# A gated linear-attention kernel: the output of one chunk and the scores of the next in one visit of the array's quarters, and a stored order of work

## The chip, the core and the metric

The kernel runs on one core of a Trainium2 chip. The metric is the device time of one execution in microseconds (us), lower is better. The core's engines work side by side and wait for each other by semaphores: TensorE (PE in the profile, PEld for its weight loads), VectorE (DVE), ScalarE (ACT), GpSimd (POOL) and SyncE (SP, which here only issues DMAs). TensorE writes its results into the banks of PSUM; the other engines take them from there.

## What is computed

The reference has two parts, one after the other.

```python
# q, k, v, alpha: (4, 8, 768, 48) = batch, heads, steps, head size
for t in range(S):
    state = alpha[:, :, t, :, None] * state + np.einsum('bhd,bhe->bhde', k[:, :, t], v[:, :, t])
    y[:, :, t] = np.einsum('bhd,bhde->bhe', q[:, :, t], state)
x = y.transpose(0, 2, 1, 3).reshape(3072, 384)
h = x @ w_in              # (384, 2048)
g = h - np.tanh(h)
out = g @ w_out           # (2048, 384)
```

The first part is a recurrence with a decay (called gla in the kernel), the second a two-layer network (moe).

## The kernel before

**Units and chunks.** The 3072 rows are cut into 12 units of 256 rows (`NU`), each into two chunks of 128 rows (`CU`). Three units make one batch element, so the state begins anew at units 0, 3, 6 and 9. Unit 0 is computed in one way (`direct`), unit 1 in halves of 64 steps with plain second products, and units 2 to 11 (`u >= PLAIN`) in halves of 64 steps with everything in the quarters of the array.

**One chunk of the recurrence** (units 2 to 11), as tasks on engines:
- `scores` (PE, L812 and L818): 16 products of `kT` and `qT`, 64x64 each, and 16 (8 in the last chunk of a batch element) products of `kn` and the values `vt`, which update the state. Contraction and output are both at most 64 wide, so each uses a quarter of the 128x128 array: one half of its rows (the contraction) and one half of its columns (the output partitions), four of them side by side. They go into the two banks of the tile `sc`, from the pool `ps_sc`, which holds one such tile.
- `masked` (DVE, L829), `mid` and `state` (DVE, L952 and L956), `decay` (DVE, L832): mask the scores into `pm`, bring the state to the chunk's middle and to its end, and decay it for the next chunk.
- `y` (PE, L885 and L895): 16 products of `qT` with the state (`state` for the first half, `mid` for the second; zeros, `none`, where the state begins anew) and 16 of `pm` with `vt`, again in quarters, into another `sc` tile.
- `x` (ACT, L922) and `rest` (DVE, L907): copy y from PSUM into `xT`, and add the part that came out in another place.
- `moves` (SP, L1021): once per unit six small DMAs that put the rows of `xT` in their last place.

**One step of the network** (eight per unit, `FS`): `first` (L1119; from unit 6 on seven products in place of eight, L1130 and L1151) multiplies `xT` with a part of `w_in` into a tile `h`. The pool `ps_h` holds two of these tiles, in turn. ACT and DVE make `g` from `h` (`square` L1162, `cube` L1171, or `keep` L1141/L1143 and `join` L1156 from unit 6 on, then L1166 and L1175), which ends with the tile `h` free again; `sums` (L1188, L1189) prepares seven products in place of eight; `second` (L1199 for units 0 and 1, L1221 after) multiplies `g` with a part of `w_out` into the output's banks. An fp32 product is executed as two matmul instructions, so the profile counts twice as many as the code issues.

**Order.** Every task is given to `Planner.add` with its engine, an assumed duration, a rank and what it must follow. `Planner.run` lists the tasks by a priority on each engine, in eight rounds, with the due times of the best round so far and, from the fifth round on, random noise on them; the best order is recorded, engine by engine, and nothing is reordered after that. Before the first output task, gaps of PE in the plan are filled with idle matmuls (`spin`, L1301), which nobody reads.

**Start.** Unit 0's and 1's inputs are turned by matmuls with the identity (`turn`, L670, 16 products of 64x128 per half of the steps), placed and scanned on DVE (L717, L736), and the weights come in 16 pieces (`fetch`, `read`, L43; ACT L86 and L87, DVE L89 and L90).

Of the kernel before, what the change touches and what calls it, by code (L numbers as in the profile page):

```python
# [9 lines left out]
FP32 = mybir.dt.float32  # L10
# [7 lines left out]
P = 128  # L18
HP = 64
CU = 2  # L20
# [301 lines left out]
class Planner:  # L322
# [5 lines left out]
    ROUNDS, SEED, NOISE = 8, 1, 2.0  # L328
    WITHIN = {"PE": 0.0, "DVE": 0.15, "ACT": 0.1}

    def __init__(self):
        self.tasks = []
        self.last = {}
        self.filler = None
        self.begin = {}

# [4 lines left out]

    def run(self, priority, before, after, late=None, begin=None):


        n = len(self.tasks)
        left = [len(before[i]) for i in range(n)]
        ready, starts, free, open_, choice = [0.0] * n, [0.0] * n, dict(begin or {}), {}, {}

        def choose(e):
            ts = open_[e]  # L350
            at = max(free.get(e, 0.0), min(ready[i] for i in ts))
            best = min((i for i in ts if ready[i] <= at), key=lambda i: (priority[i], i))
            if late:
                end = at + self.tasks[best][2]
                soon = [j for j in ts if at < ready[j] < end and late[j] < min(late[best], end)]
                if soon:
                    j = min(soon, key=lambda j: (late[j], j))
                    fits = [i for i in ts if ready[i] <= at and at + self.tasks[i][2] <= ready[j]]
                    if not fits:
                        return ready[j], e, j  # L360
                    best = min(fits, key=lambda i: (priority[i], i))
            return at, e, best
        for i in range(n):
            if not left[i]:
                open_.setdefault(self.tasks[i][1], []).append(i)
        order, stale = [], set(open_)
        while any(open_.values()):
            for e in stale:
                choice.pop(e, None)
                if open_.get(e):  # L370
                    choice[e] = choose(e)

            at, engine, i = min(choice.values())
            open_[engine].remove(i)
            starts[i] = at
            free[engine] = at + self.tasks[i][2]
            order.append(i)
            stale = {engine}
            for j, lat in after[i]:
                ready[j] = max(ready[j], free[engine] + lat)  # L380
                left[j] -= 1
                if not left[j]:
                    open_.setdefault(self.tasks[j][1], []).append(j)
                    stale.add(self.tasks[j][1])
        assert len(order) == n
        return starts, order

    def order(self):
# [10 lines left out]
        chance = random.Random(self.SEED)  # L399
        priority, late, best = [t[3] for t in self.tasks], None, None  # L400
        for n in range(self.ROUNDS):
            starts, order = self.run(priority, before, after, late if n % 2 else None, self.begin)
            ends = [s + t[2] for s, t in zip(starts, self.tasks)]
            if best is None or max(ends) <= best[0]:
                best = max(ends), starts, order
                turned, _ = self.run([-e for e in ends], after, before)
                back = [r + t[2] for r, t in zip(turned, self.tasks)]
                fair = [max(back) - b for b in back]
            late = fair if n < 4 else [x + chance.gauss(0, self.NOISE) for x in fair]
            priority = late  # L410
        _, starts, order = best
        plan = sorted(((starts[i], n, self.tasks[i][5], i) for n, i in enumerate(order)), key=lambda x: x[:2])
# [15 lines left out]
def fast(tc, q, k, v, alpha, moe_w_in, moe_w_out, out, w_in, w_out, ident, ok, pad_rows):  # L428
    nc = tc.nc
    B, H, S, D = q.shape  # L430
    NP = H // 2
# [15 lines left out]
    with ExitStack() as ctx:  # L447
# [74 lines left out]
        s_gap = raw_pool.tile([P, KT, 2 * gap], FP32, name="s_gap", bufs=1)  # L522
# [24 lines left out]
        def head(g, r):  # L547

            return 2 * g + (r + (g >= NP // 2)) % 2
# [30 lines left out]
        def load(u, what):  # L582
# [20 lines left out]
            for r in range(2):  # L603
                src = x[b].rearrange("h s d -> h (s d)")[:, t0 * D:(t0 + TU) * D]
                for g in (0, NP // 2):
                    nc.sync.dma_start(out=t[HP * r:HP * r + 32, g:g + 2].rearrange("p g t d -> p g (t d)"),
                                      in_=src[head(g, r):head(g, r) + 3:2].rearrange("g (i n) -> i g n", i=32))

        def gla(u, rank):
# [18 lines left out]
            for what, name in enumerate(("aT", "kT", "qT", "v")):  # L628
                go(f"load {name}", "SP", 1.3 if direct or what == 3 or by_matmul(u, what) else 2.2, -9 + 0.1 * what,
                   [what < 3 and u > 0 and not by_matmul(u - 1, what) and not by_matmul(u, what) and f"{name}{prev}"]  # L630
                   + [u == 1 and ("kUba 0" if what == 3 else "turn qTb 0")]
                   + [f"{last} {u - 2}.{CU - 1}" for last in ("y", "state") if what == 3 and u > 1
# [23 lines left out]
            def turn(what, n):  # L656

                if what == 2:
                    if "both" not in m:
                        m["both"] = two_banks()  # L660
                    t = m["both"][:, n]
                elif what == 1 and u == 0:
                    t = ps_h.tile([P, NP, P], FP32, name="turned", tag="h")
                else:
                    t = ps_o.tile([P, NP, P], FP32, name="turned", tag=f"o{2 * u + n}")
                m["turned", what, n] = t
                for g in range(NP):
                    for r in range(2):
                        at = (head(g, r) * CU + n) * D
                        T.matmul(t[HP * r:HP * r + HP, g, :], lhsT=rough[u, what][:, at:at + HP], rhs=ident,  # L670
                                 start=True, stop=True)

            def turned(what, n):
                return m["turned", what, n].rearrange("p g (c i) -> p g c i", c=CU)

            def place(n):
                (V.tensor_copy if n else A.copy)(tail.rearrange("p g c (i two) -> p g c i two", two=2)[:, :, :, :, n],
                                                 turned(0, n))

            def times(what, by, n, cs):  # L680

                name = ("aT", "kT", "qT")[what]
                if name not in m:
                    new(name)
                to, of = (x.rearrange("p g c (i two) -> p g c i two", two=2)[:, :, cs, :, n] for x in (m[name].rearrange("p c g t -> p g c t"), gc(m[by][:, :, 1:])))
                V.tensor_mul(to, turned(what, n)[:, :, cs], of)

            later = u > 0
            for n, ab in enumerate("ab"):
                if by_matmul(u, 0):  # L690
                    go(f"turn aT{ab}", "PE", 0.92, n * 0.1, ["load aT", later and "masked 0.0"], lambda n=n: turn(0, n))
                    go(f"aT{ab}", "DVE" if n else "ACT", 0.62, 0, [f"turn aT{ab}"], lambda n=n: place(n))
                if by_matmul(u, 1):
                    go(f"turn kT{ab}", "PE", 0.92, 1 + n * 0.1,
                       ["load kT"] + [later and x for x in ("x 0.0", "y 0.1", "state 0.1")], lambda n=n: turn(1, n))
                    for x, _, cs in parts:
                        go(f"kU{ab}{x}", "DVE", 0.33 if x else 0.6, 3, [f"turn kT{ab}", f"U{x}", n and f"kUa{x}", later and "back 0.1", later and by_matmul(u, 2) and "turn qTb"],
                           lambda n=n, cs=cs: times(1, "U", n, cs))
                if by_matmul(u, 2):
                    go(f"turn qT{ab}", "PE", 0.92, 2 + n * 0.1,  # L700
                       ["load qT"] + [later and f"qW{x}{y} 0" for x in "ab" for y in "ab"], lambda n=n: turn(2, n))
                    for x, _, cs in parts:
                        go(f"qW{ab}{x}", "DVE", 0.33 if x else 0.6, 5, [f"turn qT{ab}", f"W{x}", n and f"qWa{x}", later and "y 0.1", later and by_matmul(u, 1) and "turn kTb"],
                           lambda n=n, cs=cs: times(2, "W", n, cs))
            for what, (name, k_) in enumerate((("aT", 0), ("kT", 2), ("qT", 4))):
# [3 lines left out]
                go(name, "DVE", 1.9, k_, [f"wide {name}"] + ([f"y {u - 2}.{CU - 1}"] if u > 1 else []),  # L709
# [37 lines left out]
            def done(by, what):  # L747

                return lambda u, c=None: [f"{by}{ab}{x} {u}" for ab in "ab" for x in ("ab" if c is None else "ab"[c])
                                          if u == 0 or x == "a"] if u == 0 and by_matmul(u, what) else (  # L750
                    [f"{by}{ab} {u}" for ab in "ab"] if by_matmul(u, what) else [f"{by} {u}"])
            kU, qW = done("kU", 1), done("qW", 2)
            for x, ns, _ in parts:
                go(f"U{x}", "DVE", 1.13 if x else 2.2, 1, (["aTa", "aTb"] if by_matmul(u, 0) else ["aT"])
# [660 lines left out]
```

## Time and profile before

| what | us |
|---|---|
| three timed runs | 569.62, 570.61, 570.75; median 570.61 |
| the profiled execution, its own time | 571.14 |
| its span, from the first to the last instruction | 569.4 |
| matmuls L1119, L1130, L1151 (first product), busy | 133.1 + 130.7 + 49.4 |
| matmuls L1221, L1199 (second product), busy | 245.0 + 44.2 |
| matmuls L812, L818 (scores), busy | 15.2 + 25.2 |
| matmuls L885, L895 on sc (y), busy | 22.1 + 25.2 |

Busy times of PE rows overlap: a matmul lasts longer than the time after which the next one starts, so they add up to more than the span. The chain of waits and the timeline, where the start of the next row ends a row, show what a stretch of matmuls takes. The granted TensorE clock was 0.998 of full speed.

### The profile page before, as it was taken

Reading aid. Unit: us, or ns where it says so; the run is one execution under the profiler, and the core shown is the slowest. Engines: PE = TensorE matmul, PEld = TensorE weight load, DVE = VectorE, ACT = ScalarE, POOL = GpSimd, SP = SyncE. Lnnn points to the kernel's source line nnn. Section 1 sums busy time; section 2 is a strip of 40 time slices with the busy share of each in tenths; the row PEclk is TensorE's granted clock in tenths of the full one; section 3 lists DMA queues with packets and bytes.
Section 4 is the critical chain, followed back from the end, with each engine's and each line's share of the span. In section 5 each row is a group of like instructions: output and inputs, shape, how many; then the busy total and the mean of one; then the engine's idle time right before and its main releaser. Section 6 shows DMA issues by size and latency. Waiting matters only on the chain.

```text
span 569.4 us, 14498 instructions
## 1 busy us (share of the span) xinstructions
PE 556.5 (98%) x5881; PEld 504.2 (89%) x5881; DVE 480.8 (84%) x883; ACT 360.0 (63%) x703; POOL 4.8 (1%) x23
## 2 busy tenths in 40 slices
PE   8989999999999999999999999999999999999895
PEld 8877677778998999998999999899999999999894
DVE  6799889999998996895996999899999766776763
ACT  2788976648786676585685665585655455454650
POOL 3000000000000000000000000000000000000000
PEclk9999999999999999999999999999999999999999
DMA  7888852256652762562530311311200100100001
GB/s 192 213 246 229 283 135 62 69 122 138 145 117 77 132 159 88 120 163 91 165 103 15 91 31 29 89 32 29 62 4 1 33 5 1 35 3 0 29 1 35
DMA packets 60716, 50.88 MB, mean 89 GB/s; under 512 B 35776, under 2 KB 50400, under 8 KB 60640
## 3 DMA queue, kind: packets, MB, share of 16 engines
q1 hardware_dynamic: 57728, 48.88, 33.2%
q10 hardware_dynamic: 2912, 0.98, 0.7%
q8 instruction: 48, 0.79, 0.6%
q14 instruction: 28, 0.23, 0.2%
HBM read 44.04 MB, written 4.72 MB: 86 GB/s over the span
## 4 chain that ended last, share of the span: by engine, by line
PE 94%; DVE 2%; ACT 1%; issue 1%; DMA 1%; SPq 0%; POOL 0%; DVEq 0%; ACTq 0%; POOLq 0%
PE o L1221 32%; PE h L1119 22%; PE h L1130 13%; PE o L1199 7%; PE h L1151 7%; PE sc L812 2%; PE sc L885 2%; PE sc L818 2%; PE sc L895 2%; PE spin L1301 1%; PE sc L998 1%; PE turned L670 1%; DVE same L1280 1%; DMA raw<-in_moe_w_in_dram 1%; SPq L43 0%
## 5 line engine op out<-in xcount | busy, mean ns | idle before, releaser
L1119 PE MATMUL h<-xT,w_in 128*128 128x256 f32 x576 | 133.1, 381 | 0.8 <-ACT xT L927 0.5
L1119 PEld LDWEIGHTS h<-xT,w_in 128*128 128x128 f32 x576 | 107.5, 190 | 16.9 <-ACT xT L927 0.7
L1221 PE MATMUL o<-b,e 128*128 128x192 f32 x480 | 94.9, 326 | 0.0
L1221 PEld LDWEIGHTS o<-b,e 128*128 128x128 f32 x480 | 80.1, 190 | 0.8
L1221 PE MATMUL o<-w_out,e 128*128 128x192 f32 x320 | 79.7, 331 | 0.0
L1221 PE MATMUL o<-b,g 128*128 128x192 f32 x320 | 70.4, 326 | 0.0
L1175 DVE SCALAR_TENSOR_TENSOR g<-z,w 128x512 f32<-128x512 f32 x96 | 65.5, 684 | 4.2 <-ACT z L1166 1.2
L1143 ACT COPY u<-h 128x128 f32<-128x128 f32 x96 | 25.2, 263 | 63.1 <-PE h L1130 62.7
L1166 ACT ACTIVATE z<-u 128x512 f32<-128x512 f32 x96 | 60.4, 630 | 2.1
L1162 ACT ACTIVATE u<-h 128x512 f32<-128x512 f32 x48 | 28.4, 592 | 46.7 <-PE h L1119 46.6
L1221 PEld LDWEIGHTS o<-w_out,e 128*128 128x128 f32 x320 | 55.2, 190 | 2.3
L1130 PE MATMUL h<-xT,w_in 128*128 128x128 f32 x288 | 56.2, 280 | 1.1 <-DVE w L1156 0.9
L1130 PE MATMUL h<-xT,w_out 128*128 128x128 f32 x288 | 55.9, 276 | 1.3 <-ACT u L1141 1.3
L1221 PEld LDWEIGHTS o<-b,g 128*128 128x128 f32 x320 | 53.8, 190 | 0.2
L1156 DVE TENSOR_TENSOR w<-h,u 128x512 f32<-128x512 f32 x48 | 32.9, 686 | 23.5 <-PE h L1151 23.1
L1181 ACT ACTIVATE big<-u 128x1024 f32<-128x1024 f32 x48 | 50.3, 1049 | 0.0
L1130 PEld LDWEIGHTS h<-xT,w_in 128*128 128x128 f32 x288 | 47.5, 190 | 3.0 <-DVE w L1156 1.5
L1151 PE MATMUL h<-xT,w_in 128*128 128x256 f32 x192 | 49.4, 380 | 0.0
L1130 PEld LDWEIGHTS h<-xT,w_out 128*128 128x128 f32 x288 | 45.8, 191 | 2.1 <-ACT u L1141 1.5
L1188 DVE TENSOR_TENSOR e<-g 128x384 f32<-128x384 f32 x80 | 43.9, 549 | 1.8
L1162 ACT ACTIVATE u<-w 128x512 f32<-128x512 f32 x48 | 30.3, 630 | 23.1 <-DVE w L1156 22.2
L1199 PE MATMUL o<-w_out,g 128*128 128x384 f32 x128 | 44.2, 489 | 0.0
(158 smaller groups left out, 874.3 us busy)
## 6 DMA issues: line engine op xcount, KB each, us to landing
raw<-in_moe_w_out_dram SPq DMA_DIRECT2D x16, 768.0 KB, 4.9
raw<-in_moe_w_in_dram SPq DMA_DIRECT2D x80, 96.0 KB, 4.1
raw<-in_moe_w_in_dram SPq DMA_DIRECT2D x16, 288.0 KB, 4.7
vt<-in_v_dram SPq DMA_DIRECT2D x23, 192.0 KB, 3.7
ar<-in_alpha_dram SPq DMA_DIRECT2D x44, 96.0 KB, 3.0
kr<-in_k_dram SPq DMA_DIRECT2D x40, 96.0 KB, 2.3
qr<-in_q_dram SPq DMA_DIRECT2D x40, 96.0 KB, 2.2
out_dram<-cross SPq DMA_DIRECT2D x19, 96.0 KB, 1.7
```

The source lines that it names most:

```text
L1119: T.matmul(h[:, a, :], lhsT=w_in[:, j, f * P:(f + 1) * P], rhs=xT[u][:, j, :], start=(j == 0), stop=(j == KT - 1))
L1130: T.matmul(m["h", s][:, to], lhsT=left[n][:, s], rhs=right[u][n], start=start, stop=True, skip_group_check=True)
L1143: A.copy(m["kept", s][:, n], m["h", s][:, 3])
L1151: T.matmul(m["h", s][:, 2 * a:2 * a + 2].rearrange("p i t -> p (i t)"), lhsT=wi[:, KT - 1, s, a], rhs=xT[u][:, KT - 1, :], start=False, st ...
L1156: V.tensor_add(m["w", s], m["h", s].rearrange("p i t -> p (i t)"), m["u", s])
L1162: A.activation(m["u", s], m["h", s], AF.Square, scale=W_SCALE ** -1.5)
L1166: A.activation(m["z", s], m["u", s], AF.Square, bias=QB, scale=QA * W_SCALE)
L1175: V.scalar_tensor_tensor(out=g.rearrange("p a c t -> p (a c t)"), in0=m["z", s], scalar=QK, in1=m["w", s], op0=ALU.add, op1=ALU.mult)
L1181: A.activation(big, m["us", s // 2].rearrange("p s t -> p (s t)"), AF.Relu, bias=-U_FAST, scale=W_SCALE, accum_out=over[:, n:n + 1])
L1188: V.tensor_sub(e[:, 0:3, :], x[:, 3:4].to_broadcast([P, 3, P]), x[:, 0:3])
L1199: T.matmul(m["o"][c], lhsT=g[:, a, c, :], rhs=w_out[:, f, :], start=(f == 0), stop=(f == FT - 1))
L1221: T.matmul(o[n][:, i], lhsT=g_, rhs=w_, start=(s_ == 0 and (n, i) in ((0, 0), (1, 0), (2, 1), (3, 0))), stop=(s_ == FS - 1), skip_group_ch ...
```

## The change

1. **One visit for two tasks.** For units 2 to 11 the task `y` of a chunk is no longer a task of its own: `visit((u, c), py)` issues the y of the chunk before (`py`) together with the scores of chunk `(u, c)`. The first scores of unit 2 have no y beside them, and the y of the last chunk of all stands alone, so there are 19 joint visits. Each row half of the array has its own list, two products of one and two of the other are issued in turn: rows 64 to 127 begin with y, rows 0 to 63 end with it. Between the two parts of y that go to the same bank stands a wait for the last product of the first part.
2. **Where y goes.** Most of y goes into a tile of `ps_h`, the pool of the first product (`m["yb", c]`); the rest into columns that the scores leave free in the two banks of `sc` (`lone`). `x` is two ACT copies from the first, `rest` one DVE copy from the second, in place of two additions; `rest` no longer waits for `x`.
3. **Zero state.** Where the state begins anew, y leaves out the products with `none`.
4. **Heads.** Head `NP * r + g` takes the place of `head(g, r)` before, so both row halves write the same column halves. `products` for unit 0, `halves_products` and the loads follow.
5. **Start.** `turn` uses quarters (32 products of 64x64 per tensor instead of twice 16 of 64x128); unit 0's second y is cut into `carried` and `y`; the very first `first` is cut into two halves of 128 rows.
6. **Order.** The listing is replaced by a stored list, `STEPS`: the whole order of all tasks. The plan's times come from walking through it with the assumed durations, and are used for `spin`, of which there are 36 instead of 24. The DMAs on SP are as many as before (571); the first two pieces of `w_in` no longer stand next to each other, unit 1's inputs come between them.

```diff
-            return 2 * g + (r + (g >= NP // 2)) % 2
+            return NP * r + g
...
+        def visit(of_s, of_y):
...
+            both = two_banks()
...
+            if of_y:
+                open_y[of_y](both, work, first)
+            if of_s:
+                open_s[of_s](both, work)
+            apart = not of_s
+            (own0, y0, s0), (own1, y1, s1) = work[0], work[1]
+            rows0, rows1 = own0 + s0 + y0, y1 + own1 + s1
+            if apart:
+                rows0 = [None] * len(y1) + rows0
+            before = last = None
+            for k in range(0, max(len(rows0), len(rows1)), 2):
+                for rows, mine in ((rows1, y1), (rows0, y0)):
+                    for do in rows[k:k + 2]:
+                        if do is None:
+                            continue
+                        if mine is y0 and y0 and do is y0[0]:
+                            tc.add_manual_dep(T.nop(nofuse=True).ins, last.ins.name, mybir.DependencyInfo(
+                                mybir.DependencyClass.Sync, mybir.DependencyReason.DATA), reason="one bank, two row tiles")
+                        it = do()
+                        if mine is y1 and y1 and do is y1[-1]:
+                            last = it
...
+                def s_work(both, work):
...
+                                work[r][2].append(lambda g=g, x=x, s=s, r=r, q=q: T.matmul(
+                                    flat[r][s, g * HP:(g + 1) * HP], lhsT=m["kT"][q, c, g, s], rhs=m["qT"][q, c, g, s],
+                                    start=True, stop=True))
...
+                def y_work(both, work, begun):
...
+                    bank = m["yb", c] = ps_h.tile([P, NP, P], FP32, name="h")
...
+                    for t in range(2):
+
+                        own, ys, _ = work[t]
+                        for e in range(NP // 2):
+                            for x in range(n == 0, 2):
+                                for hh in range(2):
+                                    (own if x == t and e == 0 else ys).append(carried(t, e, x, hh))
+                        for r in range(2):
+                            for e in range(NP // 2):
+                                for hh in range(2):
+                                    (own if r == t and e == 0 else ys).append(within_(r, e, t, hh))
...
+                    if u >= PLAIN:
+
+                        t = xT[u][0:ROWS, 0:1, c * P:c * P + HP]
+                        to = bass.AP(t.tensor, t.offset, [t.ap[0], (2 * TU + HP, 2), (1, HP)])
+                        V.tensor_copy(to, m["y", c].rearrange("p r g t -> p r (g t)")[0:ROWS, :, NP * (HP + D):])
+                        return
...
-                        both = m["y", c][2]
-                        A.copy(xT[u][0:ROWS, :, to].rearrange("p (a b) t -> p a b t", a=2), both[0:ROWS, :, 0:2, :])
+                        bank = m["yb", c]
+                        A.copy(xT[u][0:ROWS, 1::2, to], bank[0:ROWS, 1::2, :])
+                        t = xT[u][0:ROWS, 0:1, c * P + HP:c * P + 2 * HP]
+                        to = bass.AP(t.tensor, t.offset, [t.ap[0], (2 * TU - HP, 2), (1, HP)])
+                        t = bank[0:ROWS, 0:1, HP:2 * HP]
+                        A.copy(to, bass.AP(t.tensor, t.offset, [t.ap[0], (2 * P - HP, 2), (1, HP)]))
...
+                    go_c("scores", "PE", 2.23 if py else 1.27, 7, kU(u, c) + qW(u, c) + [f"natural {u}", f"load v {u}"] + [x for x in held if x in plan.names()],
+                         lambda: visit((u, c), py))
...
+                    if (u, c) == (NU - 1, CU - 1):
+                        go_c("y", "PE", 1.9, 9, [f"{x} {me}" for x in ("masked", "mid", "decay")] + [f"rest {past}"], lambda: visit(None, (u, c)))
...
+                for g in range(NP):
+                    for n in range(CU):
+                        for c, x in enumerate(halves):
+                            for r in range(2):
+                                at = (head(g, r) * CU + n) * D
+                                T.matmul(m["turned", what, c][HP * r:HP * r + HP, g, :, n], lhsT=rough[u, what][x, at:at + HP], rhs=ident[x, x],
+                                         start=True, stop=True)
...
-                    go_c("y", "PE", 1.6 if n == 0 else 2.9, 9,
-                         ["masked", f"load v {u}", n > 0 and "decay", "gaps"], products)
+                    if n > 0:
+                        go_c("carried", "PE", 1.4, 8.5, ["decay", "gaps"] + qW(u, c), lambda: products(True))
+                    go_c("y", "PE", 1.6, 9, ["masked", f"load v {u}", n > 0 and "carried", "gaps"], lambda: products(False))
...
+                elif u == s == 0:
+                    add(f"first_a {me}", "PE", 1.35, r, [f"in{s}", bank, "x 0.0"], lambda: first(slice(0, P)))
+                    add(f"first {me}", "PE", 1.35, r, [f"first_a {me}", "x 0.1"], lambda: first(slice(P, TU)))
...
+        order, at = [], 0
+        for step in self.STEPS.split():
+            at += int(step)
+            order.append(at)
```

## The prediction, made before the changed kernel was run

> **What bounds the kernel.** I read the busy shares first, then the stages, then the chain of waits. The page's first row, and the table of stages (start:end, length, busy us of PE, PEld, DVE, ACT, POOL, clock, DMA share, GB/s):
>
> ```profile
> PE 556.5 (98%) x5881; PEld 504.2 (89%) x5881; DVE 480.8 (84%) x883; ACT 360.0 (63%) x703; POOL 4.8 (1%) x23
> ...
> 0.00:40.00 40.00, 36.36 (x460) 32.47 (x460) 31.05 (x60) 23.95 (x40) 4.83 (x23) 1.00 0.84 218
> 40.00:150.00 110.00, 109.97 (x1090) 83.98 (x1091) 104.52 (x173) 83.88 (x138) 0.00 (x0) 1.00 0.57 149
> 150.00:350.00 200.00, 200.00 (x2166) 185.62 (x2165) 175.82 (x325) 134.94 (x260) 0.00 (x0) 1.00 0.41 103
> 350.00:562.00 212.00, 209.60 (x2167) 201.87 (x2166) 168.25 (x327) 117.20 (x268) 0.00 (x0) 1.00 0.08 22
> ```
>
> From 40 to 562 us PE is without work for 0.03 + 0 + 2.4 us, at full clock. So there the time is the sum of what PE is given, and work of DVE and ACT counts only if PE comes to wait for it. Only the first 40 us have slack (36.36 busy, of it 8.1 idle matmuls, row L1301), and the last 7 are the output.
>
> What does a visit to the array's quarters take? Busy times overlap, so I take starts from the chain of waits (start us, us until the next piece, what):
>
> ```profile
> 42.89 0.62 PE y L885 x32
> 43.51 0.47 PE y L895 x31
> 43.98 0.47 PE sc L812 x32
> 44.45 0.45 PE sc L818 x26
> 44.90 2.78 PE o L1199 x8
> 47.68 2.59 PE h L1119 x12
> 50.27 2.58 PE o L1199 x8
> 52.85 0.62 PE y L885 x32
> 53.47 0.47 PE y L895 x31
> 53.94 2.79 PE h L1119 x12
> ...
> 93.69 0.62 PE sc L812 x32
> 94.32 0.44 PE sc L818 x26
> 94.76 2.79 PE h L1119 x12
> ```
>
> The reader is to see three visits. y alone: 53.94 - 52.85 = 1.09, and the full-array matmuls after it take 2.79 in place of 2.59, so 1.29. Scores alone: 94.76 - 93.69 = 1.07 + 0.20 = 1.27. And at 42.89, in unit 1, y and scores happen to follow each other: 44.90 - 42.89 = 2.01, + 0.20 (2.78 against 2.58) = **2.21**. Inside a visit 32 executed matmuls take 0.47, or 14.6 ns each; 0.15 is lost on entering (0.62 against 0.47) and 0.2 on leaving. Two tasks in one visit save one entry and one exit: 1.29 + 1.27 - 2.21 = 0.35. The change does by design what the order did once by chance.
>
> **The change, part by part.**
>
> *Joint visits, 19.* Each keeps all its products (the program's order shows 64, executed as 128) and saves 0.35. New is the wait of y's second part for its first, PE on itself. The order shows 16 products, 32 executed, between the two, which is 0.47 of work, while one matmul lasts 0.217 (row L895): it should be over when PE gets there. Behind it queue the last 12 products of y and 12 of the other row half, and then the network. Bounds: 0, or a full drain, 0.22 for the matmul and 0.05 for a semaphore instruction (51 ns in PE's queue rows). I take 0.05, the instruction, since the work between covers the rest: 19 x (0.35 - 0.05) = **-5.7**.
>
> [...] The new order puts two products of the same row half next to each other[...]. But L895 and L818 already run in such pairs, and take 0.47 and 0.44 for 32, no more than L812, which changes row halves each time. The row decides: no cost. [...] L885 before lets both row halves write one bank in turn, in different column halves, at full rate; now the column halves are the same. [...]
>
> *Zero state.* 24 products with zeros go, executed 48 (row "sc<-qT,none" x48): 48 x 14.6 ns = **-0.7**, at three visits.
>
> *The last y alone.* Its parts now follow each other: 12 positions with one row half, 4 with both, 12 with one. A position takes what 4 executed matmuls take side by side, 58 ns: 28 x 0.058 + 0.35 + 0.05 = 2.0 in place of 1.29: **+0.7**.
>
> *x and rest.* ACT: two copies of 112x256 and 112x128 (354 and 272 ns, row L927) in place of one of 581 (L922): +0.05 per chunk. DVE: one copy of 112x128, nearest row L912 (282), in place of 2 x 417 (L907): 20 x 0.55 = -11 us. Neither is on the path (DVE 84%, ACT 63%), so 0; DVE becomes freer, which helps the waits below.
>
> *The tile h for y.* y holds one of the two tiles until x has copied it (0.63), so first products stand closer behind the tile they take over. Adding up PE's work in the two orders between the last use of a tile and its next, the least is 3.7 us before and 2.07 now among plain steps, 1.5 in both among seven-product steps. Release needs square 0.59 and cube 0.68, or join 0.69, and hand-overs: about 1.5 and 0.9. Covered, by less: 0, and up to 0.2 per visit, 4 in all, where ACT is behind.
>
> *moves.* The last y of a unit now comes in the next unit's first visit. Its six DMAs (about 0.45 each in issue, 1.8 to landing), x, rest and from unit 6 on mix (4 x 0.29) make some 7 us; PE has 10 us of other work there where it is tightest (units 2 and 7, by the order). SP has as many DMAs as before. 0.
>
> *Order.* The gaps to win are the 2.4 above. One as the chain shows it:
>
> ```profile
> 532.89 0.56 DVE same L1280
> 533.45 0.61 DVE w L1171
> 534.06 0.03 issue
> 534.08 0.02 DVEq L1175
> 534.11 0.04 issue
> 534.15 0.70 DVE g L1175
> ```
>
> Here PE waits while DVE does the output first; 361 is like it. A longer search may remove these or open others: from -2.4 to +4; I take **-1.2**.
>
> *Start.* Followed through DVE: the turned input is complete about 0.9 earlier (one tensor of 32 quarter products in place of two halves), but the masks of unit 0 still end at about 21; its second y, shorter by the part issued before, then stands behind a turn, so its copy ends later than before (27 against 24.6), and the piece `in1` comes later on SP and DVE. On the other side three turns and unit 1's first scores lie earlier. The third first ends at about 40 in both: **-0.2**, within 2 us either way.
>
> **Sum**: -5.7 - 0.7 + 0.7 - 1.2 - 0.2 = -7.1. Span 569.4 -> 562.3, the profiled execution 571.14 -> 564.0. The timed median lies 0.5 below that execution: 570.61 -> **563.5**.
>
> **Rivals.**
> 1. *The visit drains.* If the wait costs 0.27 at all 20 places, 4.4 of the gain go: 568. For: the order of y and of the row halves has not been seen on the chip. Against: 0.47 of work between. 10%.
> 2. *The shared tile decides: slower.* ACT also has pieces of 1.05 + 0.19 (L1181). If one stands ahead of square whenever y has taken the other tile, release takes 2.7 against the least cover of 2.07, 0.65 of wait at each of 19 visits: 12.3 against 7.1 of gain, so 576. It decides from 7.1 / 19 = 0.37 per visit. Against: most covers are larger (median 7 in plain steps). 7%.
> 3. *The visits bring nothing*, because the new order opens as many gaps as they close, in the start above all: 570.5. 4%.
> 4. *More than summed*: all 2.4 of gaps go, the wait is free and the start wins 2: -7.1 - 1.2 - 1.0 - 1.8 = 559.5. 10%.
>
> **Chances.** The forecast with its own range (560 to 567) has 69%. Two executions of one kernel differ by up to 0.2%, about 1.1 us, which is no change. Faster: 69 + 10 + 10 = 89%. Same 4%, slower 7%. For 8 in 10, with rival 1 and most of 4: 559 to 568.5.
>
> **What would show it.** The chain has y and scores as one stretch of about 2.05 to 2.1, with one 2.79 (or its like) after it; no PE wait on itself of over 0.1 in a visit; PE over 99% busy from 40 us on; `rest` at 0.28. I am wrong if first products wait for cube, join or the copies x, if a visit takes over 2.4, or if the first output product starts over 2 us later than at 44.9.

## The result, and the profile after

| | us |
|---|---|
| before, four timed runs | 569.62 to 570.75, median 570.61 |
| after, four timed runs | 565.16 to 566.20, median 565.92 |
| ratio after to before | 0.9919, 95% interval 0.9902 to 0.9937 |
| forecast | 563.5, range 559.0 to 568.5 |
| span of the profiled execution, before and after | 569.4 and 564.5 |

The change makes the kernel 4.7 us faster where 7.1 were forecast. The page's first row, the row of the granted clock and the table of stages (same columns as before):

```profile
PE 553.1 (98%) x6029; PEld 502.9 (89%) x6029; DVE 463.9 (82%) x855; ACT 358.7 (64%) x723; POOL 4.9 (1%) x23
...
PEclk9989999999999999999999999999999999999998
...
0.00:40.00 40.00, 36.22 (x645) 31.51 (x646) 29.79 (x55) 19.68 (x34) 4.92 (x23) 0.96 0.77 200
40.00:150.00 110.00, 110.00 (x1139) 84.50 (x1140) 102.45 (x167) 87.98 (x147) 0.00 (x0) 1.00 0.57 155
150.00:350.00 200.00, 199.87 (x2147) 187.56 (x2147) 165.45 (x309) 131.50 (x264) 0.00 (x0) 1.00 0.41 102
350.00:557.00 207.00, 206.25 (x2099) 198.89 (x2098) 164.79 (x326) 119.53 (x280) 0.00 (x0) 1.00 0.09 24
```

From 40 us on PE is idle for 0 + 0.13 + 0.75 us, where it was 0.03 + 0 + 2.4. New is the 0.96 in the first row: the clock was not full there. The chain of waits (start, us until the next piece, what) around one joint visit:

```profile
181.99 1.08 PE h L1242 x5
183.07 0.19 PE h L975
183.27 0.05 PE h L975 x2
...
185.06 0.03 PE h L975
185.08 3.94 PE o L1344 x23
```

L975 is now y, in both of its places. From 183.07 to 185.08 are 2.01 us, and the 0.2 of leaving makes 2.21. All 16 joint visits with a state take that to within 0.01; the three where the state begins anew take 1.98, and the last y alone 2.08. Before, y took 1.29 and scores 1.26, each by itself. So 19 x (1.288 + 1.261 - 2.214) = 6.4 come from the visits, 3 x 0.23 = 0.7 from the zeros, and 0.8 are given back by the last y: **-6.3**. The gaps bring **-1.6**. These make -7.9, and the span fell by 4.9; about 3 went elsewhere. The chain at the start shows where:

```profile
33.14 0.97 DVE w_in L89
...
34.15 4.56 PE h L1242 x12
...
38.82 0.97 DVE w_in L89
...
39.84 2.86 PE h L1242 x12
42.69 0.62 PE sc L853 x32
...
44.96 2.79 PE h L1242 x12
47.74 2.58 PE o L1322 x8
```

The first output product starts at 47.74, not at 44.90: **+2.8**. The second first product (34.15) takes 4.56 us where its twins take 2.8. The trace's clock records say why: PE is at full clock from 6.94 us, at half from 34.24 to 37.66, and at full again from there to 559.90, past PE's last matmul. Before the half clock, PE had stood idle twice, for 0.37 and 1.58 us (timeline; in brackets the idle time before a row, and what ended it), the second time until the piece `in1` of the weights was converted (33.14):

```profile
31.97 0.60 PE L1121 MATMUL y<-ident,kT 112*128 112x112 f32 x4 [0.37 <-DVE kT L729]
34.15 4.54 PE L1242 MATMUL h<-xT,w_in 128*128 128x256 f32 x12 [1.58 <-DVE w_in L89]
```

The next piece was converted only when the long product was over (38.82), so the 1.7 lost there stay lost. -6.3 - 1.6 + 2.8 = -5.1, against 4.9 of the span.

### The profile page after: what moved, and what is told of

Same layout as the page of the kernel before. It is cut to its first block, busy times and chain, and to the rows that moved or that the text cites. A ratio compares the mean times of both kernels' runs of the same rounds, so it can differ in the third digit from the quotient of the medians.

```text
span 564.5 us, 14803 instructions
## 1 busy us (share of the span) xinstructions
PE 553.1 (98%) x6029; PEld 502.9 (89%) x6029; DVE 463.9 (82%) x855; ACT 358.7 (64%) x723; POOL 4.9 (1%) x23
## 4 chain that ended last, share of the span: by engine, by line
PE 94%; DVE 3%; issue 1%; ACT 0%; POOL 0%; DVEq 0%; ACTq 0%; POOLq 0%
PE o L1344 32%; PE h L1242 22%; PE h L1253 13%; PE o L1322 7%; PE h L1274 7%; PE h L975 4%; PE spin L1428 2%; PE sc L948 2%; PE sc L1121 1%; PE sc L955 1%; PE sc L975 1%; PE turned L717 1%; DVE same L1407 1%; DVE W L779 0%; DVE U L760 0%
## 5 line engine op out<-in xcount | busy, mean ns | idle before, releaser
L1242 PE MATMUL h<-xT,w_in 128*128 128x256 f32 (+1 forms) x588 | 132.9, 380 | 1.7 <-DVE w_in L89 1.6
L1242 PEld LDWEIGHTS h<-xT,w_in 128*128 128x128 f32 x588 | 109.8, 192 | 18.0 <-DVE w_in L89 2.7
L1344 PEld LDWEIGHTS o<-b,e 128*128 128x128 f32 x480 | 78.8, 191 | 0.2
L1344 PE MATMUL o<-b,g 128*128 128x192 f32 x320 | 68.4, 326 | 0.0
L1279 DVE TENSOR_TENSOR w<-h,u 128x512 f32<-128x512 f32 x48 | 32.9, 686 | 36.7 <-PE h L1274 36.7
L1253 PE MATMUL h<-xT,w_out 128*128 128x128 f32 x288 | 54.1, 275 | 0.0
L1253 PEld LDWEIGHTS h<-xT,w_in 128*128 128x128 f32 x288 | 48.4, 190 | 4.2 <-DVE w L1279 1.5
L1274 PE MATMUL h<-xT,w_in 128*128 128x256 f32 x192 | 49.0, 380 | 0.0
L1294 DVE TENSOR_TENSOR w<-h,u 128x512 f32<-128x512 f32 x48 | 32.7, 680 | 15.0 <-ACT u L1285 15.0
L1253 PEld LDWEIGHTS h<-xT,w_out 128*128 128x128 f32 x288 | 44.3, 192 | 0.1
```

The source lines that it names most:

```text
L1242: T.matmul(h[:, a, to], lhsT=w_in[:, j, f * P:(f + 1) * P], rhs=xT[u][:, j, to], start=(j == 0), stop=(j == KT - 1))
L1253: T.matmul(m["h", s][:, to], lhsT=left[n][:, s], rhs=right[u][n], start=start, stop=True, skip_group_check=True)
L1274: T.matmul(m["h", s][:, 2 * a:2 * a + 2].rearrange("p i t -> p (i t)"), lhsT=wi[:, KT - 1, s, a], rhs=xT[u][:, KT - 1, :], start=False, st ...
L1279: V.tensor_add(m["w", s], m["h", s].rearrange("p i t -> p (i t)"), m["u", s])
L1294: V.tensor_mul(m["w", s], m["h", s], m["u", s])
L1344: T.matmul(o[n][:, i], lhsT=g_, rhs=w_, start=(s_ == 0 and (n, i) in ((0, 0), (1, 0), (2, 1), (3, 0))), stop=(s_ == FS - 1), skip_group_ch ...
```

## The experiments

What was open: whether the gain is that of the visits or of the searched order; whether the wait inside a visit is free or covered; and what the start lost. All runs are set against the kernel before on the same chip, whose median was 570.98 to 571.66 there.

**The changed kernel again**, on one chip with three of the runs below (both edits together, both pieces earlier, every visit split).

> The changed kernel itself, as the base on one chip for the runs beside it. Theory A (the half clock of its profiled execution[...]): some executions are at a mean clock of 0.999 and about 1 us shorter; median 565.9. Rival B (it always happens): all executions at a clock of 0.993 to 0.994.

Measured: 565.01 (563.50 to 565.43), ratio 0.9896 (0.9874 to 0.9918). With the first four there are nine executions. Five have a mean clock of 0.993 or 0.994, and times of 565.13 to 566.20 (mean 565.7); four have 0.997 to 0.999, and 563.50 to 565.16 (mean 564.5). The one with the half clock in its records had 0.993, and 3.41 us at half of a span of 564.5 are 0.003. So by an estimate from the mean clocks the half clock comes in some executions, as theory A has it, and these take 1.2 more on the mean; why in those alone was not shown. Of the kernel before, 3 of the 37 executions beside the runs below are at 0.993 or 0.994. The execution profiled here, at 0.997, is one without the half clock at this place:

```profile
33.40 2.87 PE h L1242 x12
...
37.40 2.86 PE h L1242 x12
40.26 0.62 PE sc L853 x32
...
42.27 2.79 PE h L1242 x12
45.05 2.58 PE o L1322 x8
```

From the second first product to the third are 4.00 us, against 5.69 in the other execution: 1.69 are the half clock. The visit of unit 1 takes 42.27 - 40.26 = 2.01, against 2.27. The same two waits of PE stand before 33.40 (0.38 and 1.59 us), and here the product behind them takes 2.87.

The remaining 0.75 arise at the very start. In the first execution the records of full clock begin at 6.94 us, so most of the first turn lies before them; it takes 1.89 us there and 1.16 here (first execution, then this one):

```profile
5.28 1.89 PE L717 MATMUL turned<-ident,rough 64*64 64x64 f32 x64
```

```profile
5.19 1.16 PE L717 MATMUL turned<-ident,rough 64*64 64x64 f32 x64
```

That is 0.73, and what follows on PE keeps the lead, up to 33.40 against 34.15. The first output product starts at 45.05, about as before the change (44.90). But in the kernel before the records of full clock begin at 6.92, as late as in the first execution; with as slow a turn the changed one would be at about 45.8 (an estimate: 45.05 + 0.75). The span is 561.8, 7.6 under that of before, but it compares the fastest of nine executions with one (571.14) that was slower than the four timed ones beside it. The medians on this chip, 565.01 and 570.98, are 6.0 apart.

**Matmuls in the idle time.**

```diff
+                    for _ in range(7 if (u, s) == (0, 1) else 0):
+                        T.matmul(h[:, 0, 0:P], lhsT=ident, rhs=ident, start=True, stop=True)
                     for a in range(2):
                         f = 2 * s + a
```

> Seven matmuls of the identity stand in front of first 0:1, where TensorE was without work for 1.58 us and the clock then fell to half for 3.4 us. Theory A (the half clock is a cost of its own at the start: 12 matmuls at 380 ns in place of about 216): first 0:1 takes 2.6 in place of 4.56 us, the first output product starts about 1.9 earlier, at 45.8 in place of 47.74, and the time falls by 1.9 to 564.0. Rival B (the start is bound by the conversions of w_in on VectorE and ScalarE, whatever the clock): first 0:1 is shorter, but what follows waits for the conversions; 565.9, no change.

Measured: 564.01 (563.90 to 565.10), ratio 0.9887 (0.9864 to 0.9911), all executions at 0.997 to 0.999.

```profile
31.97 0.60 PE y L1121 x4
32.58 1.58 PE h L1240 x14
...
34.16 2.87 PE h L1244 x12
...
45.81 2.58 PE o L1324 x8
```

L1240 are the added matmuls. The product behind them starts at the same time and takes 2.87 instead of 4.56, and all that follows is 1.9 earlier (45.81 against 47.74). In the profile theory A holds. The median is 1.9 under that of the changed kernel's first four executions (565.92), but only 1.2 under that of all nine (565.16), of which only five are at 0.993 or 0.994.

**The order of unit 1's visit.** Before the change y stood ahead of the scores there, after it behind them. The edit, in the decoded order:

```diff
+        order.remove(names["y 1.0"])
+        order.insert(order.index(names["scores 1.1"]), names["y 1.0"])
```

> In unit 1 alone, y 1.0 stands before scores 1.1, as it did in the kernel before. Theory A (scores before y cost 2.46 in one visit, y before scores 2.21): the time falls by 0.25, to 565.7, and the visit at 42.6 us takes 2.21. Rival B (the 2.46 came from something else, such as the start of the row halves at different times): the visit still takes about 2.45 and the time does not move.

Measured: 564.47 (563.70 to 564.89), ratio 0.9889 (0.9871 to 0.9907), the visit 2.01 + 0.20. Theory A falls all the same: the changed kernel, with the scores first, also takes 2.01 + 0.20 when it is run again. All six executions are at 0.996 or 0.997; in the profiled one the same two waits of PE (0.37 and 1.58 us) stand before the second first product, and it takes 2.86. The 2.46 belongs to that one execution. The profiled execution of the split visits below has a long one in that place too (2.55, a visit that was not split), also behind a slow product (4.54 us); why is open.

**Both of the last two.**

> The changed kernel with two edits: seven matmuls of the identity where first 0:1 waits, and y 1.0 before scores 1.1. Theory A (each saves its own: the half clock in the executions where it falls, some 1 on the median, and 0.25): 1.2 to 1.5 below the changed kernel beside it, and all executions at 0.997 or more. Rival B (one of the two is nothing[...]): as the changed kernel less 1.0 at most.

Measured: 564.42 (563.89 to 564.85), 0.6 under the changed kernel beside it, at 0.996 to 0.999. The ratio is 0.9887 (0.9865 to 0.9909), that of the matmuls alone: the swap adds nothing, as rival B has it.

**The weight piece earlier.** `read in1` moved ahead of `sizeU 1`, `in1` ahead of `W 1`, `first 0:1` ahead of `back 1`, in the same way as above.

> The piece in1 is read and converted before the sizes and the second scan of unit 1, and first 0:1 stands before back 1. Theory A (the order of the start is what was mis-sized: in1 lands at about 25.5 us but is read only at 29, and first 0:1 starts at 34.15): first 0:1 starts at about 31, nothing runs at half clock, the first output product starts at about 45, and the time falls by 2.5 to 3, to 563. Rival B (the order only passes the wait on: unit 1's scans come 1.5 us later on VectorE and the scores of unit 1 wait in its place): 565 to 566.

Measured: 565.48 (564.08 to 566.42), ratio 0.9906 (0.9880 to 0.9932), which is the changed kernel's own. Rival B has the time right, but not what waits:

```profile
34.23 0.41 ACT kn L1135
...
36.02 1.06 ACT more L86
...
37.11 0.97 DVE w_in L89
...
38.13 4.25 PE h L1248 x12
```

`first 0:1` runs early now, but `back 1` comes behind it, so ScalarE's copy of it (L1135) comes later, and the reading of the next piece `in2` (L86) stands behind that copy in ScalarE's queue. PE waits 2.5 us for `in2`, and the product behind it takes 4.25 us where its twins take 2.86; the mean clock from 0 to 40 us is 0.97 here.

**All three edits of the start.**

> The three edits of the start together: in1 early, the seven matmuls of the identity, y 1.0 before scores 1.1. Theory A (what the start lost, 2.7 us, is order and clock, and nothing later takes it up): the first output product starts at 44.5 to 45, and the whole gain reaches the end: 563.0. Rival B (from 45 us on the kernel waits for weight pieces or for VectorE, so that an earlier start is taken up later): less than 1 of it reaches the end, over 565.

Measured: 567.51 (566.47 to 568.34), ratio 0.9940 (0.9921 to 0.9959): slower than the changed kernel. The added matmuls stand in front of `first 0:1`, which now finds its input ready, so they delay it and `back 1`, and `in2` with them: PE waits for it until 39.71, where without them it was 38.13, and the product behind takes 4.54 us. The 1.6 between are what the seven matmuls took.

**Both pieces earlier.** `read in2` ahead of `square 0:0` and `in2` ahead of `cube 0:0`, with the moves of the two orders above and no added matmuls.

> Both pieces in1 and in2 are read and converted ahead (read in1 before the sizes of unit 1, read in2 before square 0:0, so neither stands behind natural 1), first 0:1 before back 1, y 1.0 before scores 1.1. Theory A (the early order failed only because in2 stood behind natural 1 on ScalarE): first 0:1 at 31, first 0:2 at about 36, the first output product at 43 to 44 and the time 1.5 to 2 below the swap with warm clock beside it, about 562. Rival B (the start is bound by VectorE's work as a whole, so that masks, state or in3 come later by what in2 comes earlier): the first output product at 45 or later, about 564.

Measured: **562.27** (562.02 to 563.26), ratio 0.9853 (0.9831 to 0.9875), 2.7 under the changed kernel on that chip and 2.2 under the two edits. It is the fastest of all, and theory A holds. The first output product on the timeline (start, us, engine, line), in this kernel and in the changed one run beside it, the mean clock of the first 40 us 1.00 in both:

```profile
43.28 2.74 PE L1334 MATMUL o<-w_out,g 128*128 128x384 f32 x8
```

```profile
44.89 2.74 PE L1322 MATMUL o<-w_out,g 128*128 128x384 f32 x8
```

1.6 earlier, and nearly all of it reaches the end (spans 560.3 and 561.8). So the start was not bound by VectorE's work as a whole but by the order of these tasks in the queues of VectorE and ScalarE.

**Every visit split.** One matmul of the whole array stands in the middle of each of the 19 visits.

```diff
+                if k == 12 and of_s and of_y:
+                    T.matmul(flat[1][:, NP * HP:NP * HP + 16], lhsT=ident, rhs=ident[:, 0:16], start=True, stop=True)
                 for rows, mine in ((rows1, y1), (rows0, y0)):
```

> In each of the 19 joint visits one matmul of the whole array, 16 columns, stands after 48 products of the 64 or fewer, so that entering (0.15) and leaving (0.2) are paid twice; everything else, the order too, stays. Theory A (the gain of a joint visit is one entry and one exit): each visit takes 2.55 to 2.65 in place of 2.21, and the time rises by 19 x 0.35 to 0.42 = 6.7 to 8. Rival B (the visits bring little and the gain came from the searched order): under 2 more.

Measured: 574.39 (572.01 to 576.04), ratio 1.0062 (1.0044 to 1.0079), 9.4 above the changed kernel on that chip.

```profile
184.83 0.19 PE h L977
...
185.68 0.33 PE sc L632 x2
186.01 0.19 PE sc L977
186.20 0.06 PE sc L977 x2
...
187.32 2.80 PE o L1346 x16
```

The visit takes 187.32 - 184.83 = 2.49 in place of 2.01, so 0.48 more: 0.33 from the added matmul (L632) to the next one, which holds the leaving and its own work, and 0.15 for entering once more (one product takes 0.19 where the two behind it take 0.06). 19 x 0.48 = 9.1. Theory A holds: what a joint visit saves is an entry and an exit. The price is above the 0.42 given; the added matmul's own time is in it and was not measured apart. With the order unchanged, the gain is gone and more: the visits carry it.

**The wait uncovered.**

```diff
-            rows0, rows1 = own0 + s0 + y0, y1 + own1 + s1
+            rows0, rows1 = own0 + s0[:8] + y0 + s0[8:], y1 + own1 + s1
```

> In every joint visit the second part of y stands right behind the last product of the first part (8 products of the scores that stood between them come after it), so that TensorE's wait on itself has 2 products of cover in place of some 16. Theory A (the wait is a drain of one matmul and a hand-over, 0.22 + 0.05, and was free only because of the products between): each visit takes 2.4 in place of 2.21 and the time rises by 19 x 0.2 = 4, from 565.0 on this chip's kind to 569. Rival B (the wait costs nothing in any place[...]): 565, no change.

Measured: 569.73 (569.15 to 570.45), ratio 0.9964 (0.9950 to 0.9978).

```profile
182.80 0.19 PE h L975
...
183.66 0.10 PE sc L975 x4
183.76 0.05 issue
183.81 0.26 PE h L975 x2
...
185.14 3.94 PE o L1344 x23
```

At 183.76 PE waits, and the next two products take 0.26 where two of them take 0.04 elsewhere: with the issue and a longer step before it, about 0.3 more. The visit is 2.34 + 0.19 = 2.53 in place of 2.21, and 2.18 in place of 1.98 where the state is new: 16 x 0.32 + 3 x 0.20 = 5.7. The median rises by 4.7 against 565.01, but that was on another chip, and two of the five executions there are at 0.994 where all of these are at 0.997 or more; against the four of the nine at 0.997 or more (564.5) it is 5.2. So the wait is real and costs more than the 0.27 I gave for a full drain; in the changed kernel, with 16 products of the scores before it, it is free.

**The changed kernel in an order that is not searched long.** The listing of the kernel before replaces the stored list. It got one more rule, that a task takes a tile of `ps_h` only when the one two before it was given back.

```diff
+        def free_tile(i):
...
+            return len(taken) < 2 or taken[-2] in done
```

> The changed kernel's tasks, visits, tiles and turns, but the order comes from the listing of the kernel before (eight rounds, its seed and noise, with a rule added that a task takes a tile of ps_h only when the one two before it has been given back), in place of STEPS. Theory A (visits bring 6.3 of the gain by themselves, the stored order some 1.5 in the gaps, and the stored order loses at the start): visits still take 2.21, the sum of gaps after 40 us is 2 to 5 in place of 0.9, and the time is 565 to 569, still below the kernel before. Rival B (without the searched order the shared tile h makes first products wait at most visits, so that the joint visit is worth nothing without it): over 571, with first products waiting for x or cube in many places.

Measured: 595.84 (595.37 to 596.27), ratio 1.0423 (1.0406 to 1.0441). Theory A falls. Rival B has the side of 571 right, but not the cause. What PE waited for (us in total, times, longest):

```profile
PE h L1283 <- ACT u L1296: 5.0, 11, 0.7
PE sc L883 <- DVE qT L759: 4.3, 1, 4.3
PE h L1283 <- ACT u L1294: 2.9, 6, 0.8
...
PE h L1005 <- DVE w L1309: 1.2, 2, 0.6
```

The visits are not the loss: 17 of 19 take 2.21 or 1.98 as with the stored order. Two wait for a tile (last row, L1005 is y), 1.2 in all: there the shared tile holds PE up, which rival 2 of the prediction feared. Summed from start to start, the first products of units 6 to 11 take 13 us more than in the changed kernel, and the second products 10.5, most of it where such a first product follows them: a step's products wait for ScalarE's copy of the one before (L1296, L1294) with too little between them. Unit 1's start loses another 4 (second row). These sums hold a lower clock too: its mean is 0.97 from 40 to 150 us and 0.99 from 350 to 557, some 5 us by an estimate (0.03 x 110 + 0.01 x 207). So the layout needs a good order. How much of the 30 is the missing search and how much the added rule was not told apart.

## Why the prediction was right, and where it was off

- **What bounds it**: right. From 40 us on PE is idle for 0.9 us in all, and the 17 us less of DVE show in no wait of PE but the gaps counted below.
- **Joint visits** (-5.7): -6.4, and by the mechanism that was forecast: splitting the visits costs an entry and an exit each. The visit takes 2.21 as the one in unit 1 did before. The 0.05 for the wait was not paid; without its cover it is 0.32.
- **Zero state** (-0.7) and **last y** (+0.7): -0.7 and +0.8 (2.08 for 2.0).
- **x and rest** (0): `rest` takes 0.28, `x` 0.37 + 0.27, and neither is waited for.
- **Tile h** (0): in the changed kernel PE waits neither for a cube nor for a copy x. The only such wait is the one for a `join` known from 361 us, now 0.6 (0.9 before).
- **Order** (-1.2): the gaps fell from 2.4 to 0.9, -1.6. The one at 533 is gone.
- **Start** (-0.2, within 2): the term that was mis-sized. It measured +2.8 in the profiled execution, outside its bound and past the mark that the prediction set itself (2 us later than 44.9). I followed the pieces through DVE and SP and summed work, at full clock, and did not ask what a wait of PE would do to the clock: 1.7 of the 2.8 are the half clock, and 0.25 the long visit of unit 1. About 0.9 are left for the order. There the reading was off: the third `first` does not end at about 40 in either kernel. Before, the third is the one at 33.67 here, and the fourth starts at 40.03 (the row at 24.61 holds the first two):

```profile
24.61 5.45 PE L1119 MATMUL h<-xT,w_in 128*128 128x256 f32 x24 [0.47 <-ACT xT L927]
...
33.67 2.83 PE L1119 MATMUL h<-xT,w_in 128*128 128x256 f32 x12
...
40.03 2.86 PE L1119 MATMUL h<-xT,w_in 128*128 128x256 f32 x12 [0.36 <-DVE w_in L90]
```

  In the changed kernel the third starts at 39.84, and the fourth (44.96) comes behind unit 1's visit, ahead of the first output product. The copy of unit 0's second y, forecast to end at 27, ended at 29.2.
- **The sum**: with 0.9 for the start it is -6.3 - 1.6 + 0.9 = -7.0, next to the forecast's -7.1. The timed medians show less: 4.7 in the first four executions, of which three are at 0.993 or 0.994, 6.0 when run again. The four executions at 0.997 or more (564.5) are 6.1 to 6.5 under the medians of before. That the first median lies within the range is in part luck: visits and gaps gave 1.0 more than forecast, and took up a third of the 3.0 by which the start missed.
- **Rivals**: rival 1 (a drain at each visit) fell; the uncovered wait shows how it would have looked. Rival 2 (the shared tile) shows in no wait of the changed kernel. Rival 3 was right in one thing: the start did open a gap. Rival 4 had the free wait and most of the gaps right, but the start lost where it would have had to win.

## What to carry to other kernels

Work in quarters of the array paid about 0.35 us here for each stretch, not for each task: put tasks into one stretch, and put the wait that this brings behind enough other products. An order that lets TensorE wait for a piece of input can cost twice, once in idle time and once in the clock after it (here 1.58 us of idle, then 1.7 at half clock, in some executions); follow the piece through every queue it passes before moving it, since an early start behind a late copy brings nothing.

## What the runs showed of the hardware

In the clock records of the changed kernel's first profiled execution TensorE is at full clock for 27.31 us from 6.94 us on, at half for 3.41 (34.24 to 37.66) and at full for 522.24; in those of the kernel before, at full for 559.79 from 6.92 on. The timelines show PE's waits at the start, and what the 12 matmuls (128x256) of the `first` behind them take (the ends of matmuls there are modelled):

| kernel | waits of PE ahead of the product, us | it starts at | it takes, us |
|---|---|---|---|
| changed | 0.37 and 1.58 | 34.15 | 4.54 |
| split visits | 0.37 and 1.58 | 33.89 | 4.54 |
| three edits | 2.47 | 39.71 | 4.54 |
| early piece | 2.49 | 38.13 | 4.25 |
| changed, run again | 0.38 and 1.59 | 33.40 | 2.86 |
| order of unit 1's visit | 0.37 and 1.58 | 33.91 | 2.86 |
| both pieces earlier | 0.96 | 35.83 | 2.83 |
| added matmuls | 0.38 | 34.16 | 2.86 |
| before | 0.36 | 40.03 | 2.86 |

Behind the single waits of 2.47 and 2.49 us the product was slow, behind those of 0.36, 0.38 and 0.96 it was not. The same two waits of 0.37 and 1.58 had a slow product behind them in two executions and a fast one in two, so their length alone does not decide; what else does was not shown. A slow product cost up to 1.7 (4.54 against 2.86).
